# Clustered attention and two MoE layers on one core: the order of transfers and small steps within a head pair

## The chip, the cores and the metric

One core of a Trainium2 chip runs the whole program in one launch. The metric is the device time of one execution in microseconds (us), as the median of several runs. A profile of one execution stands beside it; its clock starts at the first instruction, and its span is a little shorter than the device time.

## What is computed

For 2 batches x 8 heads, 768 tokens and 64 columns per head, q and k are each assigned to one of 16 centroids of their head. Attention is allowed only inside a cluster. Two dense layers follow.

```
q_assign = argmax(q_n @ c_n.T); k_assign = argmax(k_n @ c_n.T)
mask     = q_assign[:, :, :, None] == k_assign[:, :, None, :]
scores   = where(mask, q @ k.T / 8, -1e9)
attn     = softmax(scores);  x = attn @ v          # -> [1536, 512]
x        = relu(x @ w_in) ** 2 @ w_out
out      = sum_e p[:, e] * (relu(x @ w1[e]) @ w2[e])   # p normalised, 4 experts
```

## The kernel before

**Tiles.** Attention is one loop (L1139) over 96 tiles g: 16 heads, 6 tiles of 128 queries each. Two heads make a head pair, so pair j owns tiles 12j to 12j+11. Below, "tile -5 of pair j" is tile 12j-5. All that prepares pair j is done while pair j-1 is being computed.

**Inside a tile** the order is written out by hand in ORDER (L24), one list for even and one for odd tiles. S (`products`, L1186) issues the four score matmuls of tile g+2 (`emit_S`, L586): two with the operands k1 and q1, then two, 80 rows deep, with k2 and q2. M takes the row maximum on DVE, E the exponential on ACT (L613). T0 and T1 transpose the probabilities on PE, H0 and H1 copy them out on ACT (L631), L0 and L1 form their low parts on DVE (L632). P0 and P1 multiply by v. O copies the finished block out of PSUM on ACT (L664) and, at the end of a head, sends it to the buffers xs, xo and xm with DMAs (L669, L672, L673). X1 and X2 start up to two "slot" steps on PE in the PSUM tile m, which has one buffer; Y1 and Y2 run their second halves (`finish`, L1181). R (`other`, L1169) issues the DMAs due in this tile. C runs one step of the list dq (cluster assignment: DVE maxima and POOL arithmetic, `pair_ops`, L449). K (`convert`, L1173) runs a step of converting the first layer's weights (DVE, ACT L189, POOL L191), in some tiles.

**All DMAs are issued on SP's queue**, in program order; a wait there holds everything behind it. For a pair j the steps that matter are:

- `load_pair` (L232): four DMAs bring the natural k and q of the next pair (tag nk, nq; AT "load").
- `trans_slot` (L355) at tiles -14 to -11 transposes them; ACT copies to kqf (L371), POOL forms the parts nkh, nkl, nqh, nql (L52, L373).
- `stack` (L377): "stack1" sends two DMAs into k1 (L385, L387), "stack" sends four into q1, k2 and q2. AT gives their tiles, for the even head from 12j, for the odd head from 12j+6.
- `pair_scores` (L406) at tile -10, `pair_turn` (L424) at -9 and -8, then dq steps. POOL's last one is L467.
- `pair_hot` (L473) at tile -5, in X2: three transposes (L481) of the one-hot rows; in Y2 ACT copies them to ohm (L486) and `hot_rows` (L493) issues four DMAs that put them into q2 and k2 of the even head (L498). The odd head's four follow at 12j-1. The third and fourth matmul of every S need these rows.
- `norm_steps` (L689), which finishes the pair before: f1 takes reciprocals of the row sums (DVE, L696, L697); f2 transposes them (L702), copies them (L706) and writes them to DRAM as rd (L708); f3 reads them back into rb, spread over the partitions, with two DMAs (L714); f4 adds xm to xs on POOL (L723); f5 multiplies by rb and splits (POOL, L677, L52, L686), half by half. One list entry is taken per tile from tile -10 on, behind the tile's other slot steps.

The new order of the DMAs concerns this list of SP between tiles -10 and -3 of a pair. Quoted, the steps around tile -5 (odd):

```
"S X1 E M T0 T1 Y1 H0 C P1 X2 R L0 H1 C L1 O K Y2 C"
...
while todo:
    whole(todo.pop(0))     # what is left of the tile's slot steps, at its end
```

Of the kernel before, what the change touches and what calls it, by code (L numbers as in the profile page):

```python
# [22 lines left out]

ORDER = [  # L24
    "S T0 X1 M E T1 R Y1 H0 P0 X2 C H1 L0 L1 C K Y2".split(),
    "S X1 E M T0 T1 Y1 H0 C P1 X2 R L0 H1 C L1 O K Y2 C".split()]
WARM = [12, 10, 5, 11, 3, 9]
START = {'t': [0, 0, 1, 1], 'a': [3, 3, 4, 4, 7], 'stack1': 4, 'stack': 5, 'head': 2, 'gap': 3}
AT = {"gap": 4, "stack1": -11, "stack": -9, "ohd": -7, "splitv": -3, "load": -8,
      "t": [-14, -13, -12, -11], "a": [-10, -10, -9, -8, -5], "conv": 8, "turns": (2, 6, 7, 8, 9, 10)}  # L30


# [1 line left out]
def moe_attention_kernel(  # L34
# [19 lines left out]
    B, H, S, D = q.shape  # L54
    C = centroids.shape[1]
    NT, DM = out.shape
    E = moe2_w1.shape[0]
# [148 lines left out]
    with tc.manual_schedule():  # L206
# [170 lines left out]
        def stack(i, part):  # L377
            (kh, kl), (qh, ql) = kq[i // 2, "nk"], kq[i // 2, "nq"]
            r = slice(D * (i % 2), D * (i % 2) + D)
            for nm, rows, top, low in ((("k1", 128, kh, kl),),  # L380
                                       (("q1", 128, qh, qh), ("k2", D + C, kh, None),
                                        ("q2", D + C, ql, None)))[part]:
                t = stk[i, nm] = stk_p.tile(
                    [rows, S], F32R, tag=nm, name=nm, bufs=3 if nm == "k1" else 2)
                nc.sync.dma_start(out=t[0:D].bitcast(F32), in_=top[r].bitcast(F32))  # L385
                if low is not None:
                    nc.sync.dma_start(out=t[D:2 * D].bitcast(F32), in_=low[r].bitcast(F32))  # L387
# [301 lines left out]
        def norm_steps(hp):  # L689
            st = {}  # L690

            def f1():
                sm = sums_t.pop(hp)
                r = st["r"] = sm_p.tile([128, 2, NTT], F32, tag="r", name="r", bufs=1)
                dq[:0] = [
                    lambda: nc.vector.tensor_scalar(r, sm, 1e-9, None, op0=ALU.add),  # L696
                    lambda: nc.vector.reciprocal(r, r),  # L697
                ]

            def f2():  # L700
                m = ps_m.tile([2 * NTT, 128], F32, tag="m", name="m")
                nc.tensor.transpose(m, st["r"].rearrange("p h t -> p (h t)"), identf)  # L702

                def evac():
                    rt = xs_p.tile([2 * NTT, 128], F32, tag="rt", name="rt")
                    nc.scalar.copy(rt, m)  # L706
                    rd = st["rd"] = hbm_p.tile([2 * NTT, 128], F32, tag="rd", name="rd")
                    nc.sync.dma_start(out=rd, in_=rt)  # L708
                return evac

            def f3():
                rb = st["rb"] = rb_all[:]
                for h in range(2):
                    nc.sync.dma_start(  # L714
                        out=rb[h * D:(h + 1) * D],
                        in_=st["rd"][h * NTT:(h + 1) * NTT].rearrange(
                            "t n -> (t n)").partition_broadcast(D))

            def f4():
                xm = xm_t.pop(hp)  # L720
                for c0 in range(0, S, HALF):
                    cs = slice(c0, c0 + HALF)
                    nc.gpsimd.tensor_tensor(  # L723
                        xs_t[hp][:, cs], xs_t[hp][:, cs], xm[:, cs], op=ALU.add)

            def f5(half):
                norm_scaled(hp, half, st["rb"][:, half * HALF:(half + 1) * HALF], nc.gpsimd, round_pool)

            return [f1, None, None, f2, f3, f4, lambda: f5(0), lambda: f5(1)]

        def norm_last(hp):
            st = {}
# [365 lines left out]
        early, slots = {}, {}  # L1098

        def at(d, g, f):  # L1100
            d.setdefault(max(g, 0), []).append(f)

        for i in range(1, NH):
            u0 = i * NTT
            if i > 1:
                for n, x in enumerate(("stack1", "stack")):
                    at(early, START[x] if i == 2 else u0 + AT[x], lambda i=i, n=n: stack(i, n))
                if i % 2:
                    at(early, u0 + AT["ohd"], lambda i=i: hot_rows(i))
            at(early, u0 + AT["splitv"], lambda i=i: split_v(i))  # L1110
            if i + 1 < NH:
                at(early, u0 + AT["splitv"] + 1, lambda i=i: load_v(i + 1))
        for j in range(1, NH // 2):
            u0 = 2 * j * NTT
# [18 lines left out]
        nq = []  # L1133
# [5 lines left out]
        for g in range(NU):  # L1139
            par = g % 2  # L1140
            todo = slots.pop(g, [])
            if nq:
                f = nq.pop(0)
                if f is not None:
                    todo.append(f)
            pr, w = divmod(g - 2, 2)
            has_pv = 0 <= pr < NU // 2
            end = {}

            def slot(n):  # L1150
                if todo:
                    end[n] = todo.pop(0)()

            def T(half):
                if g < NU:
                    end["H%d" % half], end["L%d" % half] = emit_T(g, half)

            def PV(half):
                if has_pv and w == half:
                    emit_PV(pr, half)  # L1160

            def PO():
                if has_pv and w == 1:
                    emit_PO(pr)
                    ii, jj = divmod(pr, NTT // 2)
                    if ii % 2 == 1 and jj == NTT // 2 - 1 and pr + 1 < NU // 2:
                        nq.extend(norm_steps(ii // 2))

            def other():  # L1169
                for f in early.pop(g, []):  # L1170
                    f()

            def convert():  # L1173
                if g >= AT["conv"] and cq:
                    if not dq and g % (2 * NTT) in AT["turns"]:
                        cq.pop(0)()
                elif not cq and g % NTT == 4:
                    for _ in range(2):
                        lq and lq.pop(0)()

            def finish(n):  # L1181
                f = end.pop(n, None)
                if f:
                    f()

            def products():  # L1186
                emit_S(g + 2)
                if g == NU - 1:
                    late.append(early_gemm1(0))

            def maximum():
                while late and g < NU - 1:
                    late.pop(0)()
                emit_max(g + 2)

            do = {
                "E": lambda: emit_exp(g + 1), "S": products,
                "M": maximum, "P0": lambda: PV(0), "P1": lambda: PV(1),
                "O": PO, "R": other, "T0": lambda: T(0), "T1": lambda: T(1),
                "X1": lambda: slot("Y1"), "X2": lambda: slot("Y2"),  # L1200
                "C": lambda: dq and dq.pop(0)(),
                "K": convert,
            }
            for a in ORDER[par]:
                do[a]() if a in do else finish(a)
            while todo:
                whole(todo.pop(0))
            while late and g == NU - 1:
                late.pop(0)()
            if g == NU - 2:  # L1210
                prep.close()
                mctx = ExitStack()
                for nm in ("w01", "g", "tp"):
                    mp[nm] = mctx.enter_context(
                        tc.tile_pool(name=nm, bufs=1, reuse_waits="tile"))
                w_pool[0, 1] = mp["w01"]
                ga = mp["g"].tile([128, 12 * TB], F32R, name="ga")
                mp["g1"] = ga.rearrange("p (k x t) -> p k x t", k=6, x=2)
                mp["g2"] = ga.rearrange("p (k t) -> p k t", t=HALF)
                fa = mp["tp"].tile([128, 6 * HALF + 1024], F32, name="fa")  # L1220
                mp["r"] = fa[:, 0:2 * TB].rearrange("p (k t) -> p k t", k=2)
                mp["c"] = fa[:, 0:6 * HALF].rearrange("p (k t) -> p k t", k=6)
                sa = fa[:, 6 * HALF:6 * HALF + 1024]
                mp["s"] = sa.rearrange("p (s k f) -> p s k f", s=4, k=2)
                cv_p.append(lambda shp: sa[:, 0:512] if len(shp) == 2 else
                            sa[:, 0:512].rearrange("p (k f) -> p k f", k=shp[1]))
# [3 lines left out]
        f1, f2, f3, f4 = norm_last(hp)  # L1230
# [152 lines left out]
```

## Time and profile before

| | |
|---|---|
| runs | 1048.63, 1047.32, 1048.61 us, median 1048.61 us |
| the profiled execution | 1047.67 us, span 1045.8 us |
| busy share of the span | PE 98%, DVE 65%, POOL 54%, ACT 51% |
| mean granted TensorE clock | 0.992 of full speed |
| attention's tiles | about 16 to 275 us of the span |
| DMAs | 88.85 MB, mean 85 GB/s |

In the profile's rows PE is the matmul engine and PEld its weight loads, DVE the vector engine, ACT the scalar engine, POOL the general one, SPq the DMA-issuing queue. A row of the timeline gives start, duration, engine, line, operation, "out<-in" and the number of merged instructions; in brackets stands how long the engine sat idle before it and what released it. A row of windows gives the stretch, its length, the busy time and instructions of PE, PEld, DVE, ACT and POOL in it, the granted TensorE clock (1.00 is full), the DMA engines' busy share and GB/s.

### The profile page before, as it was taken

The numbers are of one execution on the slowest core, as the hardware profiler recorded it, in microseconds if no ns is written. First come the engines' busy times: TensorE is split into PE (matmuls) and PEld (weight loads), VectorE is DVE, ScalarE is ACT, GpSimd is POOL, SyncE is SP. The second block draws the span as 40 slices with busy tenths as digits, with TensorE's granted clock in tenths as the row PEclk, the third lists the DMA queues.
The fourth block names the chain that finished last, engine by engine and source line by source line (L and its number), as shares of the span: only waits on it lengthen the run. The fifth ranks groups of instructions, "written<-read, shape, count | busy, mean of one in ns | idle before, by whom it ended". The sixth has DMA issues, their size and how long they took to land.

```text
span 1045.8 us, 14874 instructions
## 1 busy us (share of the span) xinstructions
PE 1020.0 (98%) x5507; PEld 907.0 (87%) x5507; DVE 676.4 (65%) x1047; ACT 531.9 (51%) x1066; POOL 567.9 (54%) x557
## 2 busy tenths in 40 slices
PE   8989888989999999999999999999999999999998
PEld 7989888989888888888888988998998998998997
DVE  8888777768876782751165655667776655655654
ACT  6888777878755543444343334334354334334331
POOL 4556676555332222225446666676678666666650
PEclk9999989999999999999999999999999999999999
DMA  4676565765022321220011221221223221221201
GB/s 118 158 178 152 129 141 133 174 158 133 17 81 81 121 81 41 81 81 6 35 41 42 80 81 41 80 81 44 78 81 104 78 81 46 76 81 48 74 1 61
DMA packets 73744, 88.85 MB, mean 85 GB/s; under 512 B 27252, under 2 KB 50184, under 8 KB 73672
## 3 DMA queue, kind: packets, MB, share of 16 engines
q1 hardware_dynamic: 73672, 87.91, 29.2%
q8 instruction: 43, 0.70, 0.3%
q14 instruction: 29, 0.24, 0.1%
HBM read 62.58 MB, written 3.19 MB: 63 GB/s over the span
## 4 chain that ended last, share of the span: by engine, by line
PE 90%; DVE 5%; DMA 2%; ACT 1%; issue 1%; POOL 1%; SPq 0%; ACTq 0%; DVEq 0%; POOLq 0%
PE bank L954 25%; PE bank L914 22%; PE bank L807 13%; PE t L626 5%; PE s L593 5%; PE bank L784 4%; PE bank L783 4%; PE bank L782 4%; PE po L640 3%; PE po L642 3%; DVE ptl L632 1%; DMA k<-ohm 1%; PE m L364 1%; DVE nb L602 1%; PE m L414 1%
## 5 line engine op out<-in xcount | busy, mean ns | idle before, releaser
L954 PE MATMUL bank<-w1h,ga 128*128 128x512 f32 x768 | 269.9, 393 | 0.0
L964 DVE SCALAR_TENSOR_TENSOR x<-bank,pe_p,x 128x512 f32<-128x512 f32 x180 | 134.9, 750 | 167.5 <-PE bank L954 167.3
L914 PE MATMUL bank<-xa,w0h 128*128 128x384 f32 x896 | 228.3, 335 | 0.1
L914 PEld LDWEIGHTS bank<-xa,w0h 128*128 128x128 f32 x896 | 164.5, 188 | 17.9 <-ACT fa L925 0.5
L954 PEld LDWEIGHTS bank<-w1h,ga 128*128 128x128 f32 x768 | 144.1, 188 | 24.5
L793 POOL TENSOR_TENSOR ga<-fa,ga 128x512 fp32r<-128x512 f32 x48 | 63.9, 1333 | 175.6 <-ACT ga L792 134.7
L954 PE MATMUL bank<-w1l,ga 128*128 128x512 f32 x384 | 151.6, 395 | 0.0
L914 PE MATMUL bank<-xa,w0l 128*128 128x384 f32 x448 | 149.7, 334 | 0.0
L925 ACT COPY fa<-bank 128x384 f32<-128x384 f32 x96 | 45.6, 475 | 171.3 <-PE bank L914 171.3
L807 PE MATMUL bank<-ga,w1h 128*128 128x512 f32 x384 | 126.5, 389 | 0.0
L934 ACT ACTIVATE ga<-fa 128x384 fp32r<-128x384 f32 x96 | 50.7, 528 | 135.5 <-DVE fa L928 135.5
L883 POOL TENSOR_TENSOR w0l<-raw,w0h 128x512 fp32r<-128x512 f32 x64 | 75.1, 1193 | 81.3 <-ACT w0h L882 81.3
L901 POOL TENSOR_TENSOR w1l<-raw,w1h 128x1024 fp32r<-128x1024 f32 x32 | 77.2, 2411 | 71.2 <-ACT w1h L900 71.2
L632 DVE TENSOR_TENSOR ptl<-t,pth 128x384 fp32r<-128x384 f32 x192 | 97.9, 549 | 26.3 <-ACT pth L631 25.8
L602 DVE TENSOR_REDUCE nb<-s 128x1 f32<-128x768 f32 x96 | 91.6, 954 | 24.7 <-PE s L593 23.4
L593 PE MATMUL s<-k,q 80*128 80x384 f32 (+1 forms) x384 | 88.7, 351 | 17.1 <-DMA k<-ohm 13.8
L937 DVE SCALAR_TENSOR_TENSOR ga<-fa,ga 128x384 fp32r<-128x384 f32 x96 | 90.5, 942 | 0.6 <-ACT ga L934 0.6
L631 ACT CAST pth<-t 128x384 fp32r<-128x384 f32 x192 | 84.4, 486 | 10.4 <-PE t L626 9.3
L613 ACT ACTIVATE p<-s,nb 128x768 f32<-128x768 f32 x96 | 87.9, 916 | 2.4 <-DVE nb L602 1.9
L626 PE MATMUL t<-identf,p 128*128 128x128 f32 x576 | 87.9, 280 | 0.4
L790 ACT ACTIVATE fa<-bank 128x512 f32<-128x512 f32 x44 | 26.4, 600 | 115.9 <-PE bank L784 115.9
L807 PEld LDWEIGHTS bank<-ga,w1h 128*128 128x128 f32 x384 | 72.0, 188 | 14.7
(213 smaller groups left out, 2057.2 us busy)
## 6 DMA issues: line engine op xcount, KB each, us to landing
raw<-in_moe_w_dram SPq DMA_DIRECT2D x64, 512.0 KB, 4.3
raw<-in_moe_w_in_dram SPq DMA_DIRECT2D x7, 1024.0 KB, 5.2
raw<-in_moe_w_out_dram SPq DMA_DIRECT2D x6, 1024.0 KB, 4.9
k<-nkh SPq DMA_DIRECT2D x28, 192.0 KB, 3.8
q<-nqh SPq DMA_DIRECT2D x28, 192.0 KB, 2.6
nv<-in_v_dram SPq DMA_DIRECT2D x16, 192.0 KB, 3.8
out_dram<-x SPq DMA_DIRECT2D x12, 256.0 KB, 2.1
k<-nkl SPq DMA_DIRECT2D x14, 192.0 KB, 3.0
```

The costliest lines, as they stand in the source:

```text
L593: nc.tensor.matmul(s[:, j, 0:HALF], stk[i, nq][:, t * 128:(t + 1) * 128], stk[i, nk][:, j * HALF:(j + 1) * HALF], start=first, stop=not first)
L602: nc.vector.tensor_reduce(out=nb, in_=s_ps[u][:, :, 0:HALF], axis=AX.XY, op=ALU.max, negate=True)
L613: nc.scalar.activation(p, s_ps.pop(u)[:, :, 0:HALF], AF.Exp, bias=nb_t.pop(u), accum_out=sums_t[hp][:, i % 2, t:t + 1])
L626: nc.tensor.transpose(tp[:, j], p_sb[u][:, half, j * 128:(j + 1) * 128], identf)
L631: return (lambda: nc.scalar.copy(dh, tp), lambda: nc.vector.tensor_tensor(dl, tp, dh.bitcast(F32), op=ALU.subtract))
L632: lambda: nc.vector.tensor_tensor(dl, tp, dh.bitcast(F32), op=ALU.subtract))
L807: nc.tensor.matmul(o, a, b, start=(ft == 0 and z == 0), stop=(ft == NF - 1 and z == 2))
L901: nc.gpsimd.tensor_tensor(lo, w, hi.bitcast(F32), op=ALU.subtract)
L914: nc.tensor.matmul(ps, w[:, o:o + 128], r_op(r, x)[:, kt], start=(first and kt == 0 and z == 0), stop=(kt == 1 and z == 2), skip_group_che ...
L937: nc.vector.scalar_tensor_tensor(out=g_t(n, f, t, 1), in0=h_src(n, f, t), scalar=0.0, in1=g_t(n, f, t, 0).bitcast(F32), op0=ALU.max, op1=A ...
L954: nc.tensor.matmul(o, a, w[:, f], start=(f == 0 and z == 0), stop=(f == 1 and z == 2))
L964: nc.vector.scalar_tensor_tensor(out=acc, in0=o, scalar=pc, in1=acc, op0=ALU.mult, op1=ALU.add)
```

## The change

Five edits, all of order:

- odd tiles run Y2 before O and K instead of behind them;
- "stack1" of an odd head moves one tile later (-10 instead of -11, counted from its own first tile, that is tile -4 of the pair instead of -5);
- `load_pair` moves two tiles sooner, from tile -8 to tile -10;
- f2 (transposing the reciprocals) moves from tile -7 to tile -8, where it is the second slot step, behind `pair_turn`;
- f4 (the additions) moves from the end of tile -5 to Y2 of tile -6; f3 and f5 stay in their tiles.

```diff
@@ -23,10 +23,10 @@
 ORDER = [
     "S T0 X1 M E T1 R Y1 H0 P0 X2 C H1 L0 L1 C K Y2".split(),
-    "S X1 E M T0 T1 Y1 H0 C P1 X2 R L0 H1 C L1 O K Y2 C".split()]
+    "S X1 E M T0 T1 Y1 H0 C P1 X2 R L0 H1 C L1 Y2 O K C".split()]
...
-AT = {"gap": 4, "stack1": -11, "stack": -9, "ohd": -7, "splitv": -3, "load": -8,
+AT = {"gap": 4, "stack1": (-11, -10), "stack": (-9, -9), "ohd": -7, "splitv": -3, "load": -10,
...
@@ -726,7 +726,7 @@
-            return [f1, None, None, f2, f3, f4, lambda: f5(0), lambda: f5(1)]
+            return [[f1], [], [f2], [], [f3, lambda: f4], [], [lambda: f5(0)], [lambda: f5(1)]]
@@ -1104,7 +1104,7 @@
-                    at(early, START[x] if i == 2 else u0 + AT[x], lambda i=i, n=n: stack(i, n))
+                    at(early, START[x] if i == 2 else u0 + AT[x][i % 2], lambda i=i, n=n: stack(i, n))
@@ -1140,9 +1140,7 @@
             if nq:
-                f = nq.pop(0)
-                if f is not None:
-                    todo.append(f)
+                todo.extend(nq.pop(0))
```

## Rows read from the trace of the kernel before

**Rows 1.** Waits of PE, whole span: us in total, times, longest us
```profile
PE s L593 <- DMA k<-ohm: 13.8, 5, 3.6
PE s L593 <- DMA q<-ohm: 3.2, 1, 3.2
```

**Rows 2.** Timeline of PE: the held score matmuls of pairs 3 and 7
```profile
111.46 0.98 PE L593 MATMUL s<-k,q 80*128 80x384 f32 x2 [3.04 <-DMA k<-ohm]
...
248.37 0.59 PE L593 MATMUL s<-k,q 80*128 80x384 f32 x2 [1.17 <-DMA k<-ohm]
```

**Rows 3.** Windows from the resumption to the fifth S after it, pairs 2, 3, 4
```profile
78.49:87.84 9.35, 9.35 (x74) 9.20 (x75) 7.17 (x12) 7.78 (x19) 8.76 (x14) 1.00 0.66 152
111.46:122.27 10.81, 10.81 (x74) 10.61 (x75) 7.36 (x12) 7.84 (x19) 8.44 (x13) 0.86 0.60 137
145.86:158.13 12.27, 12.27 (x75) 12.01 (x76) 7.36 (x12) 7.87 (x19) 8.43 (x13) 0.74 0.54 123
```

**Rows 4.** Windows of twelve tiles, from tile -2 of pairs 1 and 3
```profile
45.05:74.75 29.70, 29.65 (x224) 28.02 (x223) 26.64 (x47) 26.68 (x64) 15.49 (x20) 1.00 0.74 182
...
107.91:142.33 34.42, 31.33 (x224) 29.35 (x223) 28.26 (x48) 26.80 (x63) 22.71 (x31) 0.95 0.61 138
```

**Rows 5.** Timeline of SP's queue, tiles -8 to -5 of pair 3
```profile
95.28 1.80 SPq L245 DMA_DIRECT2D nk<-in_k_dram  x2
97.12 1.34 SPq L245 DMA_DIRECT2D nq<-in_q_dram  x2
98.56 1.09 SPq L708 DMA_DIRECT2D rd<-rt  x1
102.00 1.13 SPq L714 DMA_DIRECT2D rb<-rd  x2
103.18 0.59 SPq L385 DMA_DIRECT2D k<-nkh  x1
...
107.38 0.46 SPq L669 DMA_DIRECT2D xm<-xs  x1
107.94 0.66 SPq L498 DMA_DIRECT2D q<-ohm  x1
...
109.97 0.59 SPq L498 DMA_DIRECT2D q<-ohm  x1
```

**Rows 6.** Timeline of ACT, end of tile -5 of pair 3
```profile
103.16 0.38 ACT L664 COPY xs<-po 128x256 f32<-128x256 f32 x1 [0.17 <-PE po L642]
103.43 0.62 ACT L189 CAST w0h<-cva 128x512 fp32r<-128x512 f32 x1
103.95 0.48 ACT L486 CAST ohm<-m 128x384 fp32r<-128x384 f32 x1
```

**Rows 7.** Timeline of POOL, pair 3
```profile
101.70 0.85 POOL L467 TENSOR_SCALAR oh<-off 128x192 fp32r<-128x192 f32 x1
104.13 1.29 POOL L191 TENSOR_TENSOR w0l<-cva,w0h 128x512 fp32r<-128x512 f32 x1 [1.58 <-ACT w0h L189]
105.37 1.98 POOL L723 TENSOR_TENSOR xs<-xs,xm 128x384 f32<-128x384 f32 x2
...
122.34 1.01 POOL L373 TENSOR_TENSOR nql<-kqf,nqh 128x384 fp32r<-128x384 f32 x1
```

**Rows 8.** Timeline of PE: the one-hot transposes of pairs 3 and 7
```profile
102.96 0.37 PE L481 MATMUL m<-identr,oh 128*128 128x128 f32 x3
...
242.25 0.37 PE L481 MATMUL m<-identr,oh 128*128 128x128 f32 x3
```

**Rows 9.** Timeline of SP's queue: first one-hot DMA of pair 7
```profile
244.00 1.62 SPq L498 DMA_DIRECT2D q<-ohm  x1
```

**Rows 10.** Timelines of DVE and PE, end of tile -8 of pair 6
```profile
200.34 0.55 DVE L435 TENSOR_REDUCE A<-m 128x192 f32<-128x384 f32 x1
...
200.84 0.28 PE L642 MATMUL po<-ptl,vv 128*128 128x256 f32 x1
```

**Rows 11.** Timeline of PE: last matmul of the next pair's assignment, pair 4
```profile
125.59 0.34 PE L414 MATMUL m<-nql,cp 128*128 128x384 f32 x1
```

## The prediction, made before the changed kernel ran

> **What bounds the kernel now.** I read the waits of PE first, because PE is busy for 98% of the span and only its gaps can give much. Nearly all of them are of one kind: the score matmuls of line 593 wait for the DMAs that bring the one-hot rows into k2 and q2, 13.8 + 3.2 = 17.0 us in six waits, one for each of the pairs 2 to 7 [rows 1]. The timeline of PE places them: each time it is the third matmul of S in tile -2, the first that needs the even head's one-hot rows. Pair 3 resumes at 111.46 after 3.04 us, pair 7 at 248.37 after 1.17 us [rows 2]. So the deadline for these rows was 108.42 in pair 3 and 247.20 in pair 7.
>
> The windows behind the resumption show a second loss. The same work takes 9.35 us behind pair 2's wait, at granted clock 1.00, but 10.81 us at 0.86 behind pair 3's and 12.27 us at 0.74 behind pair 4's [rows 3]: after some waits part of the stretch ran at 1.2 instead of 2.4 GHz, for 1.46 and 2.92 us of extra time. I take pairs 5 and 6, whose waits are as long, like pair 3; pair 7's short wait I take at nothing. That is 3 x 1.46 + 2.92 = 7.3 us. Twelve tiles confirm the size: 29.70 us without a wait, 34.42 with pair 3's [rows 4], a difference of 4.72 against 3.04 + 1.46 = 4.50. Waits and clock together are worth **24.3 us**, and nothing else in attention is near that.
>
> Why are the rows late? SP's queue tells it for pair 3 [rows 5]. Natural k and q leave at 95.28 and 97.12 and take SP 3.2 us; rd follows at 98.56; rb waits for it until 102.00; the odd head's first stack (two DMAs, 0.6 each) goes at 103.18; xm waits until 107.38; only then the one-hot DMAs start, at 107.94. xm waits because its buffer is still read by the additions, which end at 105.37 + 1.98 = 107.35, and on POOL these stand behind the weight conversion's subtraction at 104.13 [rows 7]. The rows themselves had been ready since 103.95 + 0.48 = 104.43 [rows 6]. So 3.5 of the 3.6 us between ready and issued are queueing on SP, not work.
>
> **The change, part by part.**
>
> *Y2 ahead of O and K, and the odd stack1 later.* On SP the one-hot DMAs now pass xm, and the two stack1 DMAs no longer stand before them. On ACT the copy to ohm passes the block's copy and the conversion's cast. The transposes start at 102.96 and take 0.37 [rows 8]; an ACT copy began 0.17 after the PE work it waited for, and ohm takes 0.48 [rows 6]; so ohm ends at 102.96 + 0.37 + 0.17 + 0.48 = 103.98, and the first DMA can start 0.1 later (as it now follows xm's end), at 104.09. From the first issue to the resumption pair 3 took 111.46 - 107.94 = 3.52 us; pair 7 took 248.37 - 244.00 = 4.37, its first issue being stretched to 1.62 [rows 2, 5, 9]. With 3.52, pair 3 is ready at 107.61, 0.8 before its deadline. Pair 7 (and 6), with no conversion in tile -5, has a tighter one: 242.25 + 1.02 + 0.11 + 3.52 = 246.90, 0.3 before 247.20 [rows 2, 8]. With 4.37, pairs 6 and 7 would wait 0.55 each, the others 0.04. What stays is between 0 and 1.3 us; I take 0.4, nearer to the short end since no stack1 transfer is now in front.
>
> A page would set this price differently. The Trainium skill ("DMA: Bandwidth & Descriptors", Anatomy of one DMA) gives a transfer a fixed cost of about 2.0 us, most of it the receipt of the write, where the row has 111.46 - 109.97 = 1.49 us from the last issue to the resumption [rows 2, 5]. By the page's 2.0 us pairs 6 and 7 would wait 0.2 us each, an estimate inside the bounds above; its figure is for transfers that GpSimd issues.
>
> The price of the new ACT order: the block's copy used to start at 103.16, now ACT idles until ohm starts at 103.50, 0.34 us. In pairs 2 to 5 ACT runs on without a gap here [rows 6], so it may show on PE: between 0 and 7 x 0.34 = 2.4 us; I take 0.3 in those four, 1.2 us.
>
> xm now goes behind the one-hot DMAs and stack1 behind xm; neither has a reader before the next additions or tile +4 of the pair, nine tiles on. Cover gone, S of the odd head would wait.
>
> *Additions sooner.* They need no input that is late: on POOL they could start when the last one-hot step ends, 101.70 + 0.85 = 102.55, and skip the 1.58 us wait of the conversion [rows 7]. On their own they would free xm at about 104.5 instead of 107.35; with the one-hot DMAs already in front of xm they matter only to POOL's own sequence (a rival below). Nothing on the path: 0.
>
> *Next k and q sooner.* The 3.2 us of issuing move in front of the even head's four stack DMAs in tile -9. Their buffers were read last by transposes in tile -11, so SP does not wait there. The stack's reader is S in tile -2, seven tiles or some 17 us later: 0. What it gives is that rd finds SP and the DMA engines emptier.
>
> *Reciprocals a tile sooner.* rd is issued about 2 us sooner and no longer right behind the 256-byte pieces of k and q, so rb leaves before 102.00. Even unmoved, rb would be out at 102.00 + 1.13 = 103.13, ahead of 104.09 [rows 5], so this adds nothing to pairs 2 to 5 beyond what is counted. The step pays a new wait: its transpose is now second in the one PSUM tile m and must wait for DVE's reduction. In pair 6 that ends at 200.34 + 0.55 = 200.89, and PE comes there about 0.11 after 200.84 [rows 10], at the same moment. Everything behind it on PE waits too, beginning with the next S. No more than a handover, 0 to 0.3 us in six pairs, 0 to 1.8; I take 0.6 in all, since the DVE row is on time. The transpose's own PE time only moves from tile -7.
>
> **Sum.** -17.0 - 7.3 + 0.4 + 1.2 + 0.6 = -22.1 us. The profiled execution took 1047.67 us (span 1045.8), 0.9 below the median of the runs and inside them: 1047.67 - 22.1 = **1025.6 us**. The MLP behind attention is bound by PE alone and starts that much sooner.
>
> **The rivals.**
>
> 1. *POOL becomes late.* Attention gets shorter by 4.5 us a pair, but POOL's sequence (additions, conversion, two halves of the normalisation, v, four k/q parts) does not. Now it takes 107.35 to 122.34 + 1.01 = 123.35, 16.0 us with its waits [rows 7], and the next pair's last assignment matmul needs it by 125.59 [rows 11]. After, the additions end at 104.5 and the conversion near 106.3; the same 16.0 us end at 122.3, while the need moves to 125.59 - 4.50 = 121.09. If POOL's waits shrink, as they should with their inputs sooner, it is on time; if not, PE waits up to 1.2 us in five pairs: 1031.6 us. For it: POOL has hardly a gap there. Against: it is busy for only 22.71 us in a pair [rows 4].
> 2. *The one-hot rows still late*, because rb waits for rd longer than now. If rb left 3 us later than 102.00, the first one-hot DMA would start near 106.2, PE resume at 109.7, a wait of 1.3 in six pairs, too short to lower the clock by pair 7's example (I take it so): 1033.6. Against: rd leaves sooner, with 3.2 us of issuing gone from in front.
> 3. *Slower than before.* POOL works in order, and the normalisation's first multiplication waits for rb's landing. If that were late enough, v and the next k/q parts would be late and PE would wait in tile -10. It decides when the wait eats the gain, 22.1 / 6 = 3.7 us in each pair; with 0.7 us of slack rb must then land some 5 us later than today. At 5 us a pair the time is 1025.6 + 30 = 1055.6. Against: rd and rb leave sooner, as in 2.
> 4. *The change does nothing*: the one-hot DMAs wait for something else that comes as late, about 1047.7. Against: they started 0.1 us after xm's issue ended [rows 5].
>
> **How the numbers follow.** The forecast has 0.72, rival 1 0.15, rival 2 0.08, rival 3 0.03, rival 4 0.02. The forecast with every unknown at its good end is 1047.67 - 24.3 = 1023.4, with all at the bad end 1023.4 + 5.5 = 1028.9; a us lower for the spread of runs, and up into rival 1, gives 1022.4 to 1032.0. About 0.2% (2 us) is what a measurement of this kernel can tell from no change. Faster: forecast, rivals 1 and 2, 0.95; the same 0.02; slower 0.03.
>
> **What the changed profile would show.** The waits of PE lose the one-hot entries or keep under 0.6 us of each; the granted clock stays at 1.00 behind tile -2; twelve tiles take about 30 us. On SP the order in tile -5 is one-hot, xm, then stack1, the first issue 1.1 us after the transposes' start; rb leaves before them. On ACT ohm stands before the block's copy. New entries to look for: transposes of line 702 waiting for DVE's reduction, matmuls of line 414 waiting for POOL. The prediction is wrong if one-hot waits above 1 us stay, if the clock still falls, or if line 414 waits for POOL by more than 1 us a pair.

## The result, and the profile after

The changed kernel took 1029.61 us (median of 4 runs, 1028.96 to 1030.58); the kernel before, with one more run, 1047.96 us (1045.91 to 1048.63). The ratio is 0.9829, with a 95% interval of 0.9812 to 0.9846. The profiled execution took 1029.81 us, 17.86 us less than that of before, where 22.1 us less were forecast. The measured time lies inside the range.

The page of the changed kernel (span, busy shares, and the granted clock in 40 slices):

```profile
span 1028.0 us, 14886 instructions
...
PE 1015.5 (99%) x5507; PEld 899.3 (87%) x5507; DVE 675.7 (66%) x1047; ACT 530.2 (52%) x1066; POOL 567.0 (55%) x557
...
PEclk9999999999999999999999999999999999999999
```

Every slice is at nine tenths of the full clock or more, and the mean granted clock is 0.999 instead of 0.992. The waits of PE in the changed kernel, over the whole span, which answer to [rows 1]:

```profile
PE s L593 <- DMA k<-ohm: 1.4, 1, 1.4
PE m L414 <- POOL nql L373: 1.2, 3, 0.6
PE t L626 <- DVE ptl L632: 0.8, 4, 0.2
```

Of 17.0 us in six one-hot waits a single wait of 1.4 us is left, in pair 6. The two other entries are what is late next: POOL's last part of q, and DVE.

Windows of twelve tiles of the changed kernel, from tile -2 of pairs 1 and 3, which answer to [rows 4]:

```profile
45.01:75.92 30.91, 30.34 (x224) 27.92 (x223) 27.25 (x49) 26.72 (x63) 15.47 (x20) 1.00 0.82 187
107.70:138.55 30.85, 30.39 (x224) 27.80 (x223) 27.75 (x49) 26.75 (x63) 22.66 (x31) 1.00 0.69 157
```

Both readings matter. Where a one-hot wait stood in the stretch, 34.42 us became 30.85. Where none stood, 29.70 became 30.91: the change also costs 1.2 us in these twelve tiles, at full clock.

To place gain and cost I read the length of every tile of attention as the time from the start of its S on PE to the start of the next S. The 95 tiles sum to 254.93 us before and 237.33 after, 17.60 us less, which is nearly the whole result. By place within a pair:

| tiles | before to after, us | what stands there |
|---|---|---|
| -2 and the next one, pairs 2 to 7 | -3.1, -4.7, -6.2, -4.8, -3.7, -1.4: together -23.8 | one-hot waits, and the clock behind them |
| -10, summed over all pairs | 25.4 to 28.0: +2.6 (pair 3 +1.0, pair 7 +0.7, pair 2 +0.45, pair 4 +0.3) | the next pair's assignment, line 414 |
| -8, pairs 2 to 5 mainly | 2.41 to 2.96, 2.95, 2.99, 2.98: +2.3 with the rest | not forecast in this size |
| one of -4 and -3 in each of seven pairs (-4 in pairs 2 to 5, -3 in 1, 6 and 7) | about +0.2 each: +1.4 | the later copy of a block on ACT |

These four sum to -17.5 us.

**SP and ACT.** SP's queue in pair 3 of the changed kernel, tiles -8 to -5, which answers to [rows 5]:

```profile
96.39 0.96 SPq L708 DMA_DIRECT2D rd<-rt  x1
99.65 1.11 SPq L714 DMA_DIRECT2D rb<-rd  x2
103.47 0.66 SPq L498 DMA_DIRECT2D q<-ohm  x1
104.17 1.28 SPq L498 DMA_DIRECT2D k<-ohm  x2
105.49 1.05 SPq L498 DMA_DIRECT2D q<-ohm  x1
106.66 0.53 SPq L669 DMA_DIRECT2D xm<-xs  x1
107.23 0.61 SPq L385 DMA_DIRECT2D k<-nkh  x1
```

The order is the forecast one: rb first, then one-hot, xm, stack1. In pair 6 of the changed kernel the same queue reads:

```profile
190.72 0.34 SPq L708 DMA_DIRECT2D rd<-rt  x1
195.62 1.11 SPq L714 DMA_DIRECT2D rb<-rd  x2
196.82 0.66 SPq L498 DMA_DIRECT2D q<-ohm  x1
...
198.85 0.59 SPq L498 DMA_DIRECT2D q<-ohm  x1
```

and ACT's and PE's timelines there:

```profile
194.30 0.48 ACT L486 CAST ohm<-m 128x384 fp32r<-128x384 f32 x1 [0.39 <-PE m L481]
```

```profile
200.46 0.59 PE L593 MATMUL s<-k,q 80*128 80x384 f32 x2 [1.43 <-DMA k<-ohm]
```

The rows were ready at 194.30 + 0.48 = 194.78, but SP stood at rb, which waits for rd's round trip through DRAM (195.62 - 190.72 = 4.9 us from issue to issue), and sent the first one-hot DMA at 196.82, 2.0 us late. That is the wait that is left. In pair 2 rb pushes them back by 1.3 us (ready at 71.67, sent at 72.96), and PE loses 0.3.

**POOL.** Its timeline in pair 3 of the changed kernel, which answers to [rows 7]:

```profile
102.23 1.98 POOL L723 TENSOR_TENSOR xs<-xs,xm 128x384 f32<-128x384 f32 x2
104.31 1.28 POOL L191 TENSOR_TENSOR w0l<-cva,w0h 128x512 fp32r<-128x512 f32 x1
...
119.71 1.02 POOL L373 TENSOR_TENSOR nql<-kqf,nqh 128x384 fp32r<-128x384 f32 x1
```

The additions end at 104.21, as forecast (104.5). The conversion's subtraction, which stood ahead of them before, now follows and ends at 105.59. From there to the last part of q, at 120.73, POOL takes 15.1 us; the same work took 16.0 before (107.35 to 123.35). Two things hold POOL up elsewhere. In pairs 2 and 6 its normalisation waits for rb, 2.14 and 4.86 us (1.21 and 4.76 before):

```profile
75.97 1.01 POOL L677 TENSOR_TENSOR rb<-rb,xs 128x384 f32<-128x384 f32 x1 [2.14 <-DMA rb<-rd]
199.91 0.99 POOL L677 TENSOR_TENSOR rb<-rb,xs 128x384 f32<-128x384 f32 x1 [4.86 <-DMA rb<-rd]
```

And in pair 1, where no normalisation stands before it, the first part of k is written at 51.75 instead of 49.05, because the odd head's stack, whose first part now goes one tile later, still reads its buffer nkh:

```profile
51.75 0.51 POOL L52 TENSOR_SCALAR nkh<-kqf 128x384 fp32r<-128x384 f32 x1 [9.68 <-DMA k<-nkh]
```

**DVE.** In tile -10 of pair 2, a DVE step of the weight conversion and a POOL step ran as follows in the changed kernel:

```profile
58.87 1.33 DVE L178 SCALAR_TENSOR_TENSOR cva<-raw,cva 128x512 int32<-128x512 int32 x1
```

```profile
58.64 1.01 POOL L305 TENSOR_TENSOR vv<-nv,vv 128x384 fp32r<-128x384 f32 x1
```

and in the kernel before:

```profile
58.46 0.68 DVE L178 SCALAR_TENSOR_TENSOR cva<-raw,cva 128x512 int32<-128x512 int32 x1
```

```profile
56.32 1.01 POOL L305 TENSOR_TENSOR vv<-nv,vv 128x384 fp32r<-128x384 f32 x1
```

Before, POOL's split of v had ended at 57.33, ahead of DVE's step. After, the two overlap, and DVE takes 1.33 us instead of 0.68, while POOL's 1.01 stays. DVE's later steps, the row maxima of the next S among them, move with it.

### The profile page after: what moved, and what is told of

Read it like the earlier page. It is cut to its first block, busy times and chain, and to the rows that moved or that the text cites. A ratio compares the mean times of both kernels' runs of the same rounds, so it can differ in the third digit from the quotient of the medians.

```text
span 1028.0 us, 14886 instructions
## 1 busy us (share of the span) xinstructions
PE 1015.5 (99%) x5507; PEld 899.3 (87%) x5507; DVE 675.7 (66%) x1047; ACT 530.2 (52%) x1066; POOL 567.0 (55%) x557
## 4 chain that ended last, share of the span: by engine, by line
PE 85%; DVE 5%; POOL 3%; DMA 2%; ACT 2%; issue 1%; SPq 1%; POOLq 0%; ACTq 0%
PE bank L954 25%; PE bank L914 22%; PE bank L807 13%; PE bank L783 4%; PE bank L784 4%; PE bank L782 4%; PE s L593 3%; PE t L626 3%; PE po L640 2%; PE po L642 2%; DVE ptl L632 1%; DVE nb L602 1%; DMA rd<-rt 1%; DMA rb<-rd 1%; POOL nql L373 1%
## 5 line engine op out<-in xcount | busy, mean ns | idle before, releaser
L593 PE MATMUL s<-k,q 80*128 80x384 f32 (+1 forms) x384 | 85.7, 344 | 2.2 <-DMA k<-ohm 1.4
```

Of the source, the lines that this page charges most:

```text
L593: nc.tensor.matmul(s[:, j, 0:HALF], stk[i, nq][:, t * 128:(t + 1) * 128], stk[i, nk][:, j * HALF:(j + 1) * HALF], start=first, stop=not first)
```

## The experiments

My theory after the result: the new order in Y2 gives nearly all of the gain, and POOL's shifted sequence takes part of it back, at tiles -10 and -8. Rivals: the other edits carry a good part of the gain; or the costs come from f2's new place, from the place of the k and q loads, or from the order on ACT. Ratios below are to the kernel before, measured beside each run; "tile -10 sums to" means its length summed over all pairs.

### One part alone: the order of Y2, then stack1 with it

```diff
 # e1, on the kernel before
-    "... L1 O K Y2 C".split()]
+    "... L1 Y2 O K C".split()]
 # e2: e1, and
-AT = {... "stack1": -11, "stack": -9 ...
+AT = {... "stack1": (-11, -10), "stack": (-9, -9) ...
```

> The kernel before with one of the five edits alone: odd tiles run Y2 before O and K. Theory A (the one-hot DMAs were late because of what stood in front of them on SP at tile -5, xm above all): in pairs 2 to 5 the one-hot waits vanish, since rb and the odd stack1 are out by 104.4 in pair 3 and ohm is ready by 104.0; pair 6 keeps a wait of about 2.3 us because rb leaves only at 209.0 there; the tile after the odd tile -5 gets 0.2 us longer in each pair. Time about 1030 to 1033 us. Rival B (the sooner k and q loads and reciprocals are what counts): the waits of pairs 2 to 5 stay above 2 us, time 1040 us or more.

> The edit of e1 and the odd head's first stack one tile later, the three others left as before. Theory A: only pair 6 gains against e1, some 1.2 us of its wait (two DMA issues less in front), the rest is as in e1: 0.5 to 2 us below e1. Rival B: as far above 1040 us as e1.

Measured: e1 1034.91 us, ratio 0.9870 (0.9852 to 0.9888); e2 1034.71, 0.9859 (0.9839 to 0.9878). The waits of PE in e1:

```profile
PE s L593 <- DMA q<-ohm: 3.7, 1, 3.7
PE s L593 <- DMA k<-ohm: 2.5, 3, 1.1
```

One word moved in a list gives 12.7 of the 17.6 us (tiles sum to 242.21). The 3.7 us are pair 6, where rb leaves at 197.63. Pairs 2, 3 and 5 keep 1.1, 0.8 and 0.7 us, where none was expected, and the time is above the expected 1030 to 1033. With stack1 later, tile -2 of pairs 2 to 7 loses another 2.9 us (23.0 to 20.2), but tile -10 grows by 3.4 to 29.8 us: nothing is left of it in the time, where 0.5 to 2 us were expected.

### The other edits undone, one by one

```diff
 # e3, on the changed kernel: f2 back in tile -7
-[[f1], [], [f2], [], [f3, lambda: f4], [], ...
+[[f1], [], [], [f2], [f3, lambda: f4], [], ...
 # e4: the loads of k and q back in tile -8
-AT = {... "load": -10,
+AT = {... "load": -8,
 # e5: the additions back at the end of tile -5
-[[f1], [], [f2], [], [f3, lambda: f4], [], ...
+[[f1], [], [f2], [], [f3], [f4], ...
```

> The changed kernel with one edit undone: the reciprocals are transposed in tile -7 again, the first slot step there. Theory C (second in PSUM tile m of tile -8 the step makes PE and then the rest of the tile late, and gains nothing, since the transposed row leaves at nearly the same moment from tile -7): tile -8 of pairs 2 to 5 falls from 2.96 to 2.41 us, the one-hot waits stay as they are, time 1.5 to 2.5 us below the changed kernel. Rival D (the sooner reciprocals are needed): rd and rb leave 1 us or more later, pair 6 waits that much longer and POOL's waits for rb grow, time the same as or above the changed kernel's.

> The changed kernel with one edit undone: the next pair's k and q are loaded in tile -8 again. Theory A with rd as the limit: rd stands behind 3.2 us of issues and their data again, rb leaves 2 to 3 us later, pair 6 waits 3 to 4 us instead of 1.4 and may lose clock, POOL waits for rb in every pair and the assignment matmuls of line 414 wait longer: 1032 to 1037 us. Rival E (the loads' place is worth nothing, as the sum had it for pairs 2 to 5): within 1 us of the changed kernel.

> The changed kernel with one edit undone: the additions go back to the end of tile -5. Theory F (of the three edits behind Y2 and stack1, the additions are what counts, because they let POOL start its sequence before the conversion's cast): POOL's sequence is 1.3 to 2 us later in pairs 2 to 5, the assignment tile -10 grows to 4.2 to 4.9 us there as in e2, xm holds nothing up; 2 to 5 us above the changed kernel. Rival G (any one of the edits can be missing, as e3 and e4 showed): within 1 us.

Measured: e3 1030.25 us, 0.9826 (0.9807 to 0.9846); e4 1030.27, 0.9824 (0.9808 to 0.9840); e5 1032.52, 0.9860 (0.9839 to 0.9881). In e3 tile -8 still takes 2.80 to 2.83 us in pairs 2 to 5, and tile -7 grows by the 0.15 that tile -8 lost: the two together take 5.54 us with f2 in either, 5.00 before the change. So f2's new place costs nothing in sum, and tile -8's loss is not its. In e4 the time is the same; the one-hot waits change place, 1.43 us in pair 2 and 0.44 in pair 6. The longest waits of PE in e5, in sum:

```profile
PE m L414 <- POOL nql L373: 3.0, 6, 0.6
```

No one-hot wait appears there, but tile -10 sums to 32.2 us instead of 28.0, 4.2 us more, of which 2.0 come back at tile -2. The kernel is 2 to 3 us slower than the changed one (2.3 by the tiles, 2.9 by the medians; the two intervals of the ratio just overlap). So the additions' place is worth that much, through POOL's sequence, and not through xm.

### Tile -10: what POOL waits for

```diff
 # e7, on the changed kernel: second half of f5 in tile +1
+if hp < NH // 2 - 2:
+    return [[f1], [], [f2], [], [f3, lambda: f4], [], [lambda: f5(0)],
+            [], [], [], [], [lambda: f5(1)]]
 # e10: e7, and the stack sends k2's first part ahead of q1
-(("q1", 128, qh, qh), ("k2", D + C, kh, None),
+(("k2", D + C, kh, None), ("q1", 128, qh, qh),
```

> The changed kernel, and the second half of the normalisation (about 3 us of POOL) moves from tile -3 to tile +1, behind the next pair's last k/q part. Theory P (tile -10 is long because POOL is 0.1 to 1.2 us late with the k/q parts): tile -10 falls to 3.49 us in pairs 2 to 7, together 2.6 us less. Tile -8 need not change, since the moved half now runs on POOL beside the conversion step of tile -10. Time 1026.5 to 1028. Rival (tile -10 waits for something else, the odd stack's DMAs say): tile -10 stays above 3.49 in at least three pairs, time as the changed kernel.

> The kernel of e7 (second half of the normalisation in tile +1), and in the stack step the DMA that reads nkh for k2 goes first of its four. Theory T (in e7 the next pair's k parts wait no longer for POOL's work but for the landing of that odd head's DMA, which reads the single buffer they overwrite): its issue moves 1.5 to 1.8 us forward, tile -10 of pairs 2 to 7 falls to 3.49 to 3.6 us, 3 us less than e7's 27.66 for the column, 2 to 3 us off the time. Rival (something else holds tile -10): the column stays above 26.5 us.

Measured: e7 1029.93 us, 0.9827 (0.9812 to 0.9842); e10 1027.62, 0.9804 (0.9791 to 0.9817). In e7 POOL has 3 us less to do before the next pair's parts, and tile -10 still sums to 27.7 us: the first part now waits. POOL's and SP's timelines of e7, pair 6:

```profile
205.79 0.51 POOL L52 TENSOR_SCALAR nkh<-kqf 128x384 fp32r<-128x384 f32 x1 [2.74 <-DMA k<-nkh]
```

```profile
201.65 0.87 SPq L385 DMA_DIRECT2D k<-nkh  x1
```

POOL writes into a buffer that the odd head's stack still reads: its DMA into k2, issued at 201.65 behind q1's two. With that DMA first (e10) tile -10 takes 3.49 us in nearly every pair, 25.4 us in all, as before the change. So two limits lie close behind each other, POOL's sequence (with its wait for rb) and the landing of the stack's DMA that reads nkh; e7 gives 0.3 us back, both edits together 2.6. The order of the stack's DMAs alone was not run; pair 2, which e7 leaves at 3.98 us, shows that it counts by itself there. In e10 pair 2 then ran into another limit, rb in front of the one-hot rows. Its PE, SP and ACT timelines and its windows:

```profile
76.50 0.59 PE L593 MATMUL s<-k,q 80*128 80x384 f32 x2 [1.74 <-DMA k<-ohm]
```

```profile
66.94 0.39 SPq L708 DMA_DIRECT2D rd<-rt  x1
71.53 1.11 SPq L714 DMA_DIRECT2D rb<-rd  x2
72.73 0.66 SPq L498 DMA_DIRECT2D q<-ohm  x1
```

```profile
69.50 0.48 ACT L486 CAST ohm<-m 128x384 fp32r<-128x384 f32 x1 [0.40 <-PE m L481]
```

```profile
76.00:79.00 3.00, 2.50 (x13) 2.50 (x14) 0.96 (x1) 0.67 (x2) 2.83 (x4) 0.68 0.82 174
79.00:82.00 3.00, 3.00 (x20) 2.97 (x20) 2.23 (x4) 1.95 (x6) 1.83 (x4) 0.75 0.97 204
```

The rows are ready at 69.98 and leave at 72.73, behind rb. A wait of 1.74 us was followed by a granted clock of 0.68 and 0.75, part of these six us at the lower of the two levels, and the tile took 5.70 us instead of 2.41.

### Tiles -4 and -8: the order on ACT, and the conversion's place

```diff
 # e8, on the changed kernel: the block's copy first, xm's DMA at the tile's end
-"... L1 Y2 O K C".split()]
+"... L1 O Y2 K C".split()]
-nc.sync.dma_start(out=xm_t[hp][top], in_=xs_t[hp][low])
+xm_dma.append(lambda: nc.sync.dma_start(out=xm_t[hp][top], in_=xs_t[hp][low]))
...
+while xm_dma:
+    xm_dma.pop(0)()
 # e9, on the changed kernel: no conversion step in tile -10
-AT = {... "turns": (2, 6, 7, 8, 9, 10)}
+AT = {... "turns": (6, 7, 8, 9, 10, 11)}
```

> The changed kernel, and in odd tiles the block's copy goes ahead of Y2 again on ACT while its DMA into xm is issued at the end of the tile: O, Y2, K. Theory H (ACT idles 0.2 to 0.4 us before ohm, and that idle time is what lengthens tile -4 by 0.2 us in every pair): tile -4 falls from 2.42 to 2.21 and 2.28 to 2.07, ohm ends no later than now, the one-hot waits stay: 1.2 to 1.6 us below the changed kernel. Rival (ohm gets 0.3 us later and the waits eat it): tile -4 shorter, tile -2 longer, the same time.

> The changed kernel, and the conversion step of tile -10 (DVE, line 178) moves to tile -1. Theory Q (tile -8 of pairs 2 to 5 is 0.55 us longer because this step now overlaps POOL's split of v, takes 1.33 instead of 0.68 us and makes DVE late): tile -8 falls from 2.96 to 2.41 or 2.45 us as in pairs 6 and 7, 2 us less in all. Rival C of e3 (the second slot step of tile -8 itself): tile -8 stays at 2.8 us or more, the time as the changed kernel.

Measured: e8 1029.92 us, 0.9828 (0.9813 to 0.9843); e9 1030.05, 0.9830 (0.9813 to 0.9846). Both do what they should at their place: in e8 tiles -4 and -3 are as short as before the change (1.3 us less), in e9 tile -8 takes 2.44 us in pairs 2 to 7 (2.1 us less). DVE's line 178, min/median/max ns of six steps, four in attention and two behind it, first in the changed kernel, then in e9:

```profile
L178 DVE SCALAR_TENSOR_TENSOR cva<-raw,cva x6: 691/1328/1337, 58.9 to 281.5; 128x512 int32<-128x512 int32 x6
```

```profile
L178 DVE SCALAR_TENSOR_TENSOR cva<-raw,cva x6: 674/688/735, 50.4 to 281.1; 128x512 int32<-128x512 int32 x6
```

Away from POOL's split of v the step takes 688 ns again and tile -8's loss is gone. e8 shows the same without moving the step: in pair 4 it began only 0.15 us before the end of POOL's split, took 0.70 us, and tile -8 took 2.44 us there, 2.96 to 2.98 in pairs 2, 3 and 5. So the overlap is the cause. DVE's and POOL's timelines of e8, pair 4:

```profile
123.82 0.70 DVE L178 SCALAR_TENSOR_TENSOR cva<-raw,cva 128x512 int32<-128x512 int32 x1
```

```profile
122.96 1.01 POOL L305 TENSOR_TENSOR vv<-nv,vv 128x384 fp32r<-128x384 f32 x1
```

Neither run gains time. The waits of PE in e8:

```profile
PE s L593 <- DMA k<-ohm: 2.1, 2, 1.4
PE s L593 <- DMA q<-ohm: 0.9, 1, 0.9
```

In e9 pair 2's tile -2 takes 3.88 us instead of 2.75, and tile -10 sums to 29.0 instead of 28.0. In pair 2 of e9 the rows are ready at 70.92 and leave at 72.92; in the changed kernel they were ready at 71.67 and left at 72.96. What is won ahead is lost behind rb; only the 0.9 us of e8 are pair 3, where rb was out in time and the two one-hot issues to k2 took 2.00 us instead of 1.28.

### The limit behind rb

```diff
 # e6, on the changed kernel: weight loads away from the stretch between rd and rb
-at(early, 2 * NTT + kk, lambda kk=kk: load_in(kk))
+at(early, 2 * NTT - 2 + kk, lambda kk=kk: load_in(kk))
-elif not cq and g % NTT == 4:
+elif not cq and g % (2 * NTT) in (0, 10):
 # e11: e6 + e8 + e9 + e10 together
 # e12: e11 without e6; rb's loads behind the odd stack, f5 whole in tile +1
+return [[f1], [], [f2], [], [lambda: None, lambda: f4], [], [], [],
+        [f3], [], [], [lambda: f5(0), lambda: f5(1)]]
```

> The changed kernel, with the first layer's weight loads taken off the stretch before rd: the four pieces of tiles 12 to 15 go in tiles 10 to 13, the pieces of tile -8 go in tile 0 of a pair. Theory R (what is left of the one-hot waits, in pairs 2 and 6, is rb, which waits on SP for rd, and rd's landing stands behind the weight pieces' data): in pair 6 rb leaves 1.5 us or more sooner than rd + 4.9 us, its wait of 1.4 us goes; in pair 2 the first tile falls from 2.75 to 2.41; POOL's waits for rb shrink and with them tile -10 of pairs 3 and 7: 2 to 3.5 us below the changed kernel. Rival S (rd's landing does not depend on what is queued before it): rb leaves 3 to 5 us behind rd as now, the same time.

> The changed kernel with everything at once: block's copy first on ACT with xm's DMA at the tile's end (e8), conversion step of tile -10 to tile -1 (e9), weight loads away (e6), second half of the normalisation later and nkh's DMA first (e10). If the theories hold side by side (no one-hot waits, tile -10 at 3.5, tile -8 at 2.44, tile -4 at 2.07 to 2.25), the attention tiles lose 1.3 + 2.1 + 2.1 + 2.4 us or so against the changed kernel: 1021 to 1024 us. If what one wait gives back another takes, as in e8 and e9 alone, 1027 us or more.

> The kernel of e11 with the weight loads back in their place, and rb's two DMAs moved from tile -6, ahead of the one-hot DMAs, to tile -2, behind the odd head's stack; both halves of the normalisation run in tile +1, behind the next pair's k/q parts. Theory U (what is left of the one-hot waits is rb, which holds SP's queue 3 to 5 us for rd's landing, in pairs 2 and 6 beyond the moment ohm is ready, and whose 384 KB then stretch the one-hot issues): no one-hot wait above 0.4 us is left in any pair, tile -10 stays at 3.5 us, tile -8 at 2.44, and the time falls to 1020 to 1023 us, the fastest of all. Rival V (the waits left are the landing of the one-hot DMAs themselves, or POOL is now too late with both halves): waits of 1 us or more stay in pairs 2, 3 or 6, or tiles -9 to -6 grow, and the time stays at 1027 us or more.

Measured: e6 1030.51 us, 0.9836 (0.9820 to 0.9851). Moving the weights doesn't bring rb nearer to rd; in pair 6 rd left at 191.01 and rb at 196.06. e11: 1029.39, 0.9819 (0.9805 to 0.9832). Against the changed kernel all four edits together are worth nothing that can be measured, since rb still stands in front of the one-hot rows; the waits of PE in e11:

```profile
PE s L593 <- DMA q<-ohm: 4.4, 3, 2.0
```

Pairs 2 and 6 have 2.0 and 1.6 of it, behind rb; the 0.8 of pair 3 come from a stretched issue, as below.

e12: **1026.17 us** (5 runs), 0.9785 (0.9770 to 0.9800), faster than both kernels. The waits of PE, and SP's queue in pair 2:

```profile
PE t L626 <- DVE ptl L632: 1.0, 3, 0.5
PE po L640 <- DVE xs L659: 0.8, 1, 0.8
PE s L593 <- DMA k<-ohm: 0.5, 1, 0.5
```

```profile
67.19 0.41 SPq L708 DMA_DIRECT2D rd<-rt  x1
70.14 0.66 SPq L498 DMA_DIRECT2D q<-ohm  x1
...
79.25 1.58 SPq L714 DMA_DIRECT2D rb<-rd  x2
```

With nothing waiting in front, the one-hot rows leave at 70.14 instead of 72.73 in e10, and the cures count: the tiles sum to 233.89 us. (e12 moves the first half of the normalisation too; its share was not taken apart.) It is still 3 to 6 us above the 1020 to 1023 I expected. Tile -2 keeps 0.5 to 0.8 us too much in pairs 2 to 4; in pair 3 the issue of the one-hot DMAs to k2 took 2.50 us for two, where 1.28 was seen above, and PE waited 0.49. In pair 2 the overlap of DVE and POOL is back in another place: POOL's split of v, no longer behind the normalisation, now runs beside an earlier step of the conversion, which takes 1.23 us instead of the 0.43 in e11, and PE waits 0.53 us for DVE behind it. DVE's and POOL's timelines of e12:

```profile
72.87 1.23 DVE L167 TENSOR_SCALAR cva<-raw 128x512 int32<-128x512 int32 x1
```

```profile
72.81 1.01 POOL L305 TENSOR_TENSOR vv<-nv,vv 128x384 fp32r<-128x384 f32 x1
```

Pair 4 has it too (0.97 us). The late normalisation has a price as well: in tile +4 of pair 7 PE waited 0.8 us for DVE, DVE 1.2 us for POOL, and the tile took 3.21 us instead of 2.18. Tiles -8, -5 and -4 grew by 0.2 to 0.6 us in some of pairs 4 to 6; their cause was not looked for by a run and stays open.

## Why the prediction was right, and where its sum was off

The time was 4.2 us above the forecast of 1025.6 in the profiled execution, inside the range, by the mechanism named. Term by term, from the tiles:

| term | forecast | measured |
|---|---|---|
| one-hot waits and the clock behind them | -17.0 - 7.3 = -24.3 | -25.8 (-23.8 gained, 2.0 left) |
| what stays of the waits | +0.4 | +2.0 (pair 6 1.7, pair 2 0.3) |
| the block's copy later on ACT | +1.2 | +1.4 |
| f2's new place | +0.6 | 0: tile -7 loses what tile -8 gains (e3) |
| additions sooner, loads sooner, POOL's sequence | 0 | +2.6 at tile -10, +2.3 at tile -8 |

The 4.2 us are nearly all in the last row.

**The queue on SP** was read rightly, and e1 shows it by itself. The step that failed is "rb would be out at 102.00 + 1.13 = 103.13, ahead of 104.09": it rested on pair 3 alone. In pairs 3, 4, 5 and 7 it held. In pair 6 rb left 4.9 us behind rd and pushed the one-hot DMAs back by 2.0, in pair 2 by 1.3, which is rival 2's mechanism in two pairs. The kernel before already showed it for pair 6, where the rows were ready at 208.18 + 0.48 = 208.66 and rb left after that (SP's and ACT's timelines):

```profile
209.01 1.13 SPq L714 DMA_DIRECT2D rb<-rd  x2
```

```profile
208.18 0.48 ACT L486 CAST ohm<-m 128x384 fp32r<-128x384 f32 x1
```

e12 shows it from the other side. (Between ready and issued pair 3 has 107.94 - 104.43 = 3.5 us, not the 3.6 of the prediction; nothing rests on it.)

**The waits and the clock** were worth 1.5 us more than forecast, and hardly for the clock. Behind the resumption pairs 5 and 6 took 10.89 and 10.92 us to the fifth S, nearly pair 3's 10.81 [rows 3], so the clock's term was 7.5 instead of 7.3. The rest is in the held tile: pair 2's took 5.86 us at full clock, 0.23 more than its wait of 3.22 and the 2.41 of a tile that is not held, and each of the six pairs has as much. The prediction's twelve tiles, 4.72 against 4.50, had shown this remainder. That it balanced the waits that stayed (1.6 us more than forecast) is chance.

**f2.** The forecast looked for the cost of tile -8 in the transpose that waits for DVE's reduction. Tile -8 did get longer, but e3 put f2 back and tile -8 stayed long, and no wait of line 702 appears among PE's; e9 found the cause in DVE's conversion step beside POOL's split of v. The sum had no term for that, because it took POOL's later position against PE as free of charge for DVE.

The Trainium skill has this rule ("SBUF — State Buffer", SBUF: two separate sides): VectorE and GpSimd share a pair of ports, held by one instruction to its end, and a VectorE operation with two inputs in SBUF has to wait for a GpSimd operation that reads SBUF and began first. The rows agree: POOL began first, at 58.64, and ended at 59.65; DVE's step ended 0.55 us later, hardly less than the 0.68 it takes alone.

**POOL.** Rival 1 had a chance of 0.15 as a case of its own, "PE waits up to 1.2 us in five pairs". It came in a small size on top of the forecast, 2.6 us over all pairs, and belonged in the sum. Its step "If POOL's waits shrink, as they should with their inputs sooner" held in part: in pair 3 they shrank by 0.9 us, where 1.2 were needed, and tile -10 of pair 4 grew by 0.3. More came from what the sum had not looked at. The waits for rb in pairs 2 and 6 did not shrink, and tile -10 of the next pairs, 3 and 7, grew by 1.0 and 0.7 us; that these waits are the reason is read from the trace, and no run moved them alone. And nkh is held longer by the later stack1: pair 2's tile -10 takes 3.50 us in e1, 3.90 in e2 and 3.50 in e10, which sends that DMA sooner. The prediction asked for the readers of what stack1 writes and not for the next writer of what it reads.

**Additions sooner** were costed at 0, "they matter only to POOL's own sequence". e5 shows that this sequence was by then on the path: 2 to 3 us. **Loads sooner** and **reciprocals sooner** at 0 for the gain held (e4, e3). **The odd stack1** moved, with the order of Y2 alone, gains at tile -2 and loses as much at tile -10 (e2); the forecast had not kept its share apart.

Rivals 3 and 4 fell as cases of their own: no wait took the gain's place, and the one-hot DMAs left as soon as SP was free. Rival 3's mechanism, POOL waiting for rb, is inside the 2.6 us.

## What to carry to other kernels

When a wait at the front of a queue goes, ask pair by pair, and not in one example, what comes to stand in front next; here it was the round trip rd to rb, and as long as it stood there, what was cured elsewhere (e8, e9) gave nothing, nor did all edits together (e11). When PE gets faster by several us a pair, every in-order engine beside it is shifted against it by as much: cost that shift, for buffers it frees late and for the neighbours it now overlaps. A cure that shortens its own tile and not the kernel is no failure: look for the deadline that it moved forward.

## What the runs showed of the hardware that was not expected

- A DVE operation with two inputs in SBUF took 1.33 us instead of 0.68 beside a POOL operation, whose own 1.01 us did not change (changed kernel, pair 2); where only the last 0.15 us of POOL's operation overlapped (e8, pair 4) it took 0.70. A DVE operation with one input took 1.23 us instead of 0.43 beside the same POOL operation (e12, pair 2).
- Waits of PE for the one-hot rows of 1.17 us (before, pair 7) and 1.43 us (after, pair 6) were followed by a granted clock of 1.00; one of 1.74 us (e10, pair 2) by 0.68 and 0.75 in two windows of 3 us. Yet the 3.22 us of pair 2 before the change were followed by 1.00 [rows 3], so the length of a wait alone did not decide.
- A tile whose S was held took 0.23 us more than its wait and an unheld tile together, at a granted clock of 1.00 (before, pair 2).
- rb followed rd by 2.1 to 5.1 us on SP's queue in pairs 2 to 7, for the same few KB through DRAM, in the kernels that keep rb there; moving the weight loads out of the way did not shorten it (e6). Why it varies is open.
